# Bucketed attention with a gated product on one core: raw tokens in tiles of their own, and queries scaled by -1/8 on GpSimd so that a score pass is one minimum

## The chip, the core and the metric

The kernel runs on one core of a Trainium2 chip. The metric is the device time of one execution in microseconds (us). The engines: PE (TensorE) multiplies matrices and is fed weights by PEld; DVE (VectorE), ACT (ScalarE) and POOL (GpSimd) work elementwise; SP (SyncE) here only issues transfers (DMAs). Each engine takes its instructions in the order in which the program lists them, and waits on semaphores for the other engines and for DMAs. SBUF is the working memory on the chip, PSUM the memory that matmuls write.

## What is computed

Attention over 4 batches of 8 heads, 768 tokens and 64 dimensions, in which a query sees only keys of its own bucket, and then a gated product over all 3072 tokens:

```python
q_bits = (np.einsum('bhsd,dk->bhsk', q, proj) > 0)      # 6 bits; k likewise
mask = q_bucket[:, :, :, None] == k_bucket[:, :, None, :]
scores = (1 / 8) * np.matmul(q, k.transpose(0, 1, 3, 2))
scores = np.where(mask, scores, -1000000000.0)
attn = np.exp(scores - scores.max(-1)); attn = attn / (attn.sum(-1) + 1e-9)
x = (attn @ v) as [3072, 512]
out = (sigmoid(x @ w_gate) * (x @ w_val)) @ w_out       # 512 -> 1536 -> 512, weights in float64
```

## The kernel before

**Attention stage.** Sixteen pairs of heads (`pair`), each in two groups of three query tiles (`group`). `load` fetches q, k and v of a pair through SP's queue; `turn` transposes q and k on PE; `high` and `low` split each into a coarse and a fine float32r part, so that three matmuls give full precision; `hash_` multiplies by the projection, and `bits_q` and `bits_k` turn signs into +-1 rows, those of q times 2^34 (`HALF`, in `mul_q`). `scores` adds the product of these rows to q.k in PSUM, so that a pair of different buckets ends far below zero. `maximum` (L1048) is one DVE pass per query tile and head out of PSUM: it writes the scores times -1/8 to `e` in SBUF and accumulates their minimum into `st`. Two small DVE operations per query tile follow, for both heads at once: `scale_` (L1056) makes the exponential's factor, -1, or 0 for a row in which everything is masked, and `bias_` (L1060) makes its bias, the minimum or 0. `exponent` (L1067, ACT) takes exp(scale * e + bias) with the row's sum. Then transposes (L1100), copies out of PSUM (L1107, on ACT or DVE), products with v (L1117), the division (`divided`, L1127, POOL) and a store to `xd` in DRAM. Beside this run the conversion of the float64 weights (`load_w`, `load_pair`, `floats`: a DMA, DVE, ACT and POOL operations), and with two blocks of weights the first part of the gated product (`moe_early`, L537 and L570), whose sums go to `part` in DRAM.

**Late stage.** `products` does the other ten blocks, in pairs `jp` 1 to 5, batch after batch. A batch makes ten visits (`visit`), alternately for gate (g) and value (v). A visit is a seven-product scheme (L784): seven operands x0 to x6 made of the batch's tokens (halves of the features by halves of the tokens: B11, B12, B21, B22, and four differences), each times one of seven weight sums; the results build up in PSUM banks A, B and D and are read in between by ACT copies (`copies`, L792) and DVE additions (`summed`, L799). After a v visit, ACT and DVE make the gated values and six pieces of the product with w_out (L570) are put between the next visits' products. The weight sums of a visit (1.8 MB) stream from DRAM through POOL's queue (`fetch_stream`, L1217) into three slots. The last pair's weights (`jp` 5) are not converted in the attention stage but during batch 0 of the late one.

**The operands before.** Each operand X[n] is a tile with two halves, coarse and fine. The tokens of x0 and x1 are loaded (L652) into the place of their own fine half (`raw`), those of B12 and B22 into `xb` (L657); the differences go to `xt0` to `xt2` or over `xb` (L664). An ACT cast makes the coarse half (L669), a DVE subtraction the fine one (L672). The tiles are given back by the last visit of the batch: x0's after its first product, x2's and x3's together (`x`) after its last.

**The order.** All work is listed as tasks with a key, an engine, an estimated duration and counted resources (`stock`: tiles and banks). `Plan.order` plays the tasks through in time and emits them in that order; this becomes the order of every engine's queue. A DMA task is expected to land a fixed 2.0 us plus its bytes at 240 bytes per ns after its issue (0.6 us), or when its queue's wire is free. Any change of a duration or a resource can change the order everywhere.

## Time and profile before

| | before |
|---|---|
| median of 3 runs | 1084.75 us (1080.46 to 1087.05) |
| the profiled execution's own time | 1079.3 us |
| its span, first to last instruction | 1077.5 us |
| mean granted TensorE clock | 0.988 of full speed |
| busy PE / DVE / ACT / POOL | 1024.9 / 697.8 / 567.1 / 202.8 us |
| moved by DMA | 196.38 MB |

The profile is of one execution. Busy time counts an engine's instructions; TensorE's instructions are pipelined and their ends modelled, so that records overlap and a busy PE need not be PE at its peak. A row of the timeline gives start, length, engine, line, operation, output and inputs, and in brackets how long the engine had been idle and what ended that. A row of a group gives the count, then the total and mean length, then the idle time before its instructions and what ended most of it. In the chain of waits each piece is work that the end of the execution can be followed back to. Stretches of time are in us from the first instruction.

### The profile page before, as it was taken

The page shows a single profiled execution, that of the slowest core. Times are in us where ns is not written, and L with a number is a line of the kernel's source. Part 1 is how long each engine was busy: PE and PEld are TensorE (multiplying, and loading weights), DVE is VectorE, ACT ScalarE, POOL GpSimd, SP SyncE. Part 2 cuts the span into 40 slices and gives each one's busy share as a digit, 9 for nine tenths or more (in the row PEclk, how much of TensorE's full clock was granted, in tenths as well). Part 3 has the DMA queues.
Part 4 walks back from the last instruction along what each step waited for, and adds up shares of the span by engine and source line. Part 5 has one row for each costly group of instructions (what it writes and reads, how often), then busy time and mean ns, then how long its engine had stood idle before and what let it go on. Part 6 is the DMA issues. An engine that isn't in the chain of part 4 may idle for free.

```text
span 1077.5 us, 20497 instructions
## 1 busy us (share of the span) xinstructions
PE 1024.9 (95%) x8169; PEld 811.4 (75%) x8172; DVE 697.8 (65%) x1464; ACT 567.1 (53%) x1011; POOL 202.8 (19%) x230
## 2 busy tenths in 40 slices
PE   9999898999999999989999899999998999979998
PEld 5665566676675766656677789889997999879997
DVE  6898978889989778987746673464236333444333
ACT  2777776777786776857635433333234232422331
POOL 0013235344442423422031000000000000000000
PEclk9999998999999999999999999999999999989999
DMA  8345364764766456553168796466435743565521
GB/s 205 84 133 154 113 199 134 252 189 153 231 192 198 155 179 195 191 170 113 39 230 290 272 328 242 166 231 228 166 137 214 260 180 137 180 220 196 189 85 59
DMA packets 114561, 196.38 MB, mean 182 GB/s; under 512 B 61217, under 2 KB 83745, under 8 KB 109345
## 3 DMA queue, kind: packets, MB, share of 16 engines
q1 hardware_dynamic: 108544, 121.66, 36.0%
q0 software_dynamic: 5760, 73.40, 18.5%
q8 instruction: 64, 1.05, 0.4%
q14 instruction: 33, 0.26, 0.1%
q10 hardware_dynamic: 160, 0.00, 0.0%
HBM read 140.51 MB, written 41.94 MB: 169 GB/s over the span
## 4 chain that ended last, share of the span: by engine, by line
PE 77%; DVE 12%; DMA 6%; ACT 3%; issue 2%; POOL 1%; SPq 0%; ACTq 0%; DVEq 0%; POOLq 0%
PE y L570 13%; PE pv L1117 10%; PE sc L1034 8%; PE zBg L784 7%; PE zBv L784 7%; PE tp L1100 5%; PE zDg L784 4%; DVE e L1048 3%; PE zDv L784 3%; PE zo L570 3%; PE zg L537 3%; PE zv L537 3%; PE sc L1039 2%; PE zAg L784 2%; DMA x<-xd 2%
## 5 line engine op out<-in xcount | busy, mean ns | idle before, releaser
L1067 ACT ACTIVATE e<-e,st 128x768 f32<-128x768 f32 x192 | 196.5, 1026 | 71.6 <-DVE st L1060 71.5
L1048 DVE TENSOR_SCALAR_CACHE_REDUCE e<-sc 128x768 f32<-128x768 f32 x192 | 178.0, 951 | 21.8 <-PE sc L1039 21.2
L570 PE MATMUL y<-wo,gh 128*128 128x512 f32 x480 | 152.2, 399 | 0.0
L1117 PE MATMUL pv<-ef,vr 128*64 128x384 f32 x768 | 142.0, 499 | 0.0
L1100 PEld LDWEIGHTS tp<-ident,e 64*128 64x128 f32 x2304 | 85.5, 140 | 36.0 <-issue 20.2
L784 PE MATMUL zBv<-x,wsv 128*128 128x384 f32 x480 | 98.6, 340 | 9.9 <-ACT t167v L792 5.8
L570 PEld LDWEIGHTS y<-wo,gh 128*128 128x128 f32 x480 | 91.1, 190 | 15.7
L1100 PE MATMUL tp<-ident,e 64*128 64x64 f32 x2304 | 97.2, 227 | 5.3 <-ACT ef L1107 1.8
L784 PE MATMUL zBg<-x,wsg 128*128 128x384 f32 x480 | 97.3, 337 | 5.1 <-ACT t167g L792 3.7
L784 PEld LDWEIGHTS zBv<-x,wsv 128*128 128x128 f32 x480 | 86.5, 191 | 17.1 <-ACT t167v L792 7.4
L1107 ACT COPY ef<-tp 128x768 f32<-128x768 f32 x107 | 83.4, 792 | 25.5 <-PE tp L1100 25.2
L1034 PE MATMUL sc<-kh,ql 64*128 64x384 f32 x192 | 86.0, 448 | 9.2 <-DVE e L1048 2.9
L570 PE MATMUL y<-wo,gl 128*128 128x512 f32 x240 | 94.4, 393 | 0.0
L784 PEld LDWEIGHTS zBg<-x,wsg 128*128 128x128 f32 x480 | 85.7, 189 | 11.2 <-ACT t167g L792 4.4
L877 ACT CAST gh<-zt 128x384 fp32r<-128x384 f32 x80 | 41.0, 514 | 100.9 <-DVE zt L872 83.4
L1034 PE MATMUL sc<-kh,qsl 64*128 64x384 f32 x192 | 86.0, 448 | 7.1 <-DVE ef L1107 3.8
L1107 DVE COPY ef<-tp 128x768 f32<-128x768 f32 x85 | 80.4, 950 | 18.7 <-PE tp L1100 18.5
L1117 PEld LDWEIGHTS pv<-ef,vr 128*64 128x64 f32 x768 | 48.4, 137 | 52.5 <-issue 48.0
L1127 POOL TENSOR_TENSOR xs<-xs,rb 128x384 f32<-128x384 f32 x32 | 34.5, 1079 | 182.5 <-DVE xs L1124 117.6
L1039 PE MATMUL sc<-kb,qb 64*128 64x384 bf16 x384 | 65.2, 335 | 0.0
L1034 PE MATMUL sc<-kh,qsh 64*128 64x384 f32 x192 | 64.4, 335 | 0.0
L1034 PE MATMUL sc<-kl,qh 64*128 64x384 f32 x192 | 64.3, 335 | 0.0
(194 smaller groups left out, 2092.5 us busy)
## 6 DMA issues: line engine op xcount, KB each, us to landing
wsg<-kzg POOLq DMA_DIRECT2D x20, 1792.0 KB, 7.7
wsv<-kzv POOLq DMA_DIRECT2D x20, 1792.0 KB, 8.2
kzg<-wkg SPq DMA_DIRECT2D x10, 896.0 KB
kzv<-wkv SPq DMA_DIRECT2D x10, 896.0 KB
kr<-in_k_dram SPq DMA_DIRECT2D x64, 96.0 KB
qr<-in_q_dram SPq DMA_DIRECT2D x32, 192.0 KB
vr<-in_v_dram SPq DMA_DIRECT2D x16, 384.0 KB
qsh<-qh SPq DMA_DIRECT2D x32, 192.0 KB
```

Source lines behind the costliest of these rows:

```text
L537: nc.tensor.matmul(z["acc"][:, :GN], a[:, wc], x[xx][:, c, :], start=(c == 0 and i == 0), stop=(c == KC - 1 and i == 2),)
L570: nc.tensor.matmul(acc, a[:, slot, ts_], w, start=(first and i == 0), stop=(last and i == 2))
L784: nc.tensor.matmul(acc, streams[n, jp][:, c, wa, a_], X[x_][:, xa, c], start=first and c == 0 and i == 0, stop=c == 1 and i == 2, skip_gro ...
L877: nc.scalar.copy(side["h"][:, blk], w["z", blk])
L1034: nc.tensor.matmul(sc[:, j, :GN], q_[rows, c], z["k" + x][rows, h * GN : (h + 1) * GN], start=(m == 0), stop=False, tile_position=(j * D, 0),)
L1039: nc.tensor.matmul(sc[:, j, :GN], z["qb"][rows, c], z["kb"][rows, h], start=False, stop=True, tile_position=(j * D, 0),)
L1048: nc.vector.tensor_scalar(sp(e), gz["sc", t, h][:, :, :GN], -SCALE, None, op0=ALU.mult, op1=ALU.min, accum_out=gz["st", t][:, 0, h : h + 1],)
L1067: nc.scalar.activation(e, e, AF.Exp, bias=st[:, 2, h : h + 1], scale=st[:, 1, h : h + 1], accum_out=gz["su"][:, h * GT + t : h * GT + t + 1],)
L1100: nc.tensor.transpose(tp[:, r, at_ : at_ + D], gz["e", t, h][rows, c * P : (c + 1) * P], ident[rows, rows], tile_position=(r * D, 0),)
L1107: copy(gz["ef", c].rearrange("p (n r d) -> p r n d", r=2, d=D), gz["tp", c][:, :, :GN].rearrange("p r (n d) -> p r n d", d=D),)
L1117: nc.tensor.matmul(gz["pv"][rows, :GN], z["v"][:, h, c], gz["ef", c][:, h * GN : (h + 1) * GN], start=(c == 0), stop=(c == NC - 1), tile_p ...
L1127: nc.gpsimd.tensor_mul(gz["xs"], gz["xs"], gz["rb"])
```

## The change

*The score pass.* A new task, `scaled_q`, multiplies the loaded queries in place by -1/8 on POOL, between the load and the transposes. The projection for the queries is multiplied by -8 in turn, and the sign of `mul_q` is reversed, so that the scores come out of PSUM already times -1/8, with masked ones above 1e9. `maximum` now takes the minimum with 1e9 and accumulates the minimum, which is the bias; `scale_` and `bias_` are gone, the exponential's scale is the constant -1, and it waits for its own head's pass alone. Every scaling is by a power of two.

*Raw tokens.* B11, B21 and the difference T2 get tiles `r0`, `r1`, `r2`, B12 and B22 stay in `xb`; T3, T1 and T4 are written over B12, B11 and B21. Operand tiles are taken only by the casts, and x2 and x3 are given back one by one. The token loads no longer wait for the last conversions of the batch before (`in_turn["x"]`).

*Tiles and planner.* `ob`, `raw2` and `t` get one tile more each; the last two blocks of w_out go to the early blocks' tiles (`home`) and wait for the early part's last matmuls (`g_free`); the late pairs are loaded ahead of the late blocks of w_out. In the planner, transfers on the two queues slow each other, and two kinds of DMA get 3 us of `slack` on their landing.

```diff
...
-                        self.wire[e] = max(self.wire[e], free[e]) + t.size / RATE
-                        t.tail = max(t.tail, self.wire[e] + LANDING - free[e])
+                        other = "sp" if e == "pool" else "pool"
+                        begin, alone = max(self.wire[e], free[e]), t.size / RATE
+                        both = max(0, self.wire[other] - begin)
+                        takes = alone + min(alone, both / 2)
+                        self.wire[e] = begin + takes
+                        self.wire[other] += min(both, takes) / 2
+                        t.tail = max(t.tail, self.wire[e] + LANDING + t.slack - free[e])
...
-    nc.vector.tensor_scalar(mul_q, mul_q, -HALF, None, op0=ALU.mult)
+    nc.vector.tensor_scalar(mul_q, mul_q, HALF, None, op0=ALU.mult)
...
-                nc.vector.tensor_scalar_mul(w[rows, at_ : at_ + NB], praw[rows], sign)
+                nc.vector.tensor_scalar_mul(w[rows, at_ : at_ + NB], praw[rows], sign / -SCALE if n == "q" else sign)
...
-        ef=4, raw1=1, mid1=1, raw2=1, mid2=1, wk=1, xr=1, x=1, ob=2,
-        t=0, zt=0, ws0=0, ws1=0, ws2=0, xb=0, xt0=0, xt1=0, xt2=0, x1=0, x4=0, x5=0, x6=0, wk2=0,
+        ef=4, raw1=1, mid1=1, raw2=2, mid2=1, wk=1, xr=1, x2=1, x3=1, ob=3,
+        t=0, zt=0, ws0=0, ws1=0, ws2=0, xb=0, r0=0, r1=0, r2=0, x1=0, x4=0, x5=0, x6=0, wk2=0,
-    late_stock = dict(wk2=1, y=6, t=2, zt=3, xt0=1, xt1=1, xt2=1, ws1=1, ws2=1, xb=1, x1=1, x4=1, x5=1, x6=1)
+    late_stock = dict(wk2=1, y=6, t=3, zt=3, r0=1, r1=1, r2=1, ws1=1, ws2=1, xb=1, x1=1, x4=1, x5=1, x6=1)
...
-    def dma(key, nbytes, emit, engine="sp", **kw):
+    def dma(key, nbytes, emit, engine="sp", slack=0, **kw):
-        t.size = nbytes
+        t.size, t.slack = nbytes, slack
...
-        a = dma(key, 524288, load_, after=after, take=[place])
+        a = dma(key, 524288, load_, slack=3000 if last else 0, after=after, take=[place])
...
+    def home(j):
+        early = j if j < J1 else j - NJ + J1 if j >= NJ - J1 else None
+        pool, tag = (later["w"], f"wo{j}") if early is None else (w1, f"wo{early}")
+        return pool.tile([P, 2, N_EL], F32R, name=f"wo{j}", tag=tag)
...
-            w = later["w"].tile([P, 2, N_EL], F32R, name=f"w{n}{j}", tag=f"w{n}{j}")
+            w = home(j)
-        h = add(key, "act", 560, high, after=[e], take=[] if early or last else ["wk"])
+        h = add(key, "act", 560, high, after=[e] + (g_free if last else []), take=[] if early or last else ["wk"])
...
-                FIRST, "act", 415, lambda c=c: high(c), after=[a, prev], take=["x"] if c == 0 else []
+                FIRST, "act", 415, lambda c=c: high(c), after=[a, prev], take=["x2", "x3"] if c == 0 else []
...
-                take=z["bank"] if c == 0 else [], give=(["x"] + (["ws0"] if last == "end" else [])) if last and c == KC - 1 else [],
+                take=z["bank"] if c == 0 else [], give=(["x2", "x3"] + (["ws0"] if last == "end" else [])) if last and c == KC - 1 else [],
...
+        RAW = dict(B11="r0", B21="r1", T2="r2")
+        R = {}
+        def raw(n):
+            R[n] = later["w"].tile([P, 2, GN], F32, name=f"{n}_{b}", tag=RAW[n])
+            return R[n]
+        def load_first(n, h):
...
+            both = later["w"].tile([P, 2, 2, GN], F32, name=f"xb_{b}", tag="xb")
+            R["B12"], R["B22"] = both[:, 0], both[:, 1]
...
+                nc.sync.dma_start(both[:, h], xd_(h, 1))
...
+            X[n] = (xp if n in TAG else later["w"]).tile(HALF_X, F32R, name=f"{n}_{b}", tag=TAG.get(n, n))
+            nc.scalar.copy(X[n][:, 0], R[of])
+        def low(n, of):
+            nc.vector.tensor_sub(X[n][:, 1], R[of], f(X[n])[:, 0])
+        was = [a for g in range(NG) for a in stored[b, g]]
+        l0 = dma(FIRST, 393216, lambda: load_first("B11", 0), after=was, take=["r0"])
...
+        l1 = dma(FIRST, 393216, lambda: load_first("B21", 1), after=was, take=["r1"])
...
+        def dve(emit, after, take=(), give=()):
+            return add(FIRST, "dve", 930, emit, after=after, take=list(take), give=list(give))
+        def operand(n, of, after, give=()):
+            h = add(FIRST, "act", 830, lambda: high(n, of), after=after, take=["xr" if n == "x0" else n])
+            ready[n] = dve(lambda: low(n, of), [h], give=give)
+        def t3():
+            R["T3"] = R["B12"]
+            nc.vector.tensor_sub(R["T3"], R["B22"], R["B12"])
+        def t2():
+            nc.vector.tensor_add(raw("T2"), R["T3"], R["B11"])
+        def t1():
+            R["T1"] = R["B11"]
+            nc.vector.tensor_sub(R["T1"], R["B22"], R["T2"])
+        def t4():
+            R["T4"] = R["B21"]
+            nc.vector.tensor_sub(R["T4"], R["B21"], R["T2"])
+        d3 = dve(t3, [lb])
+        d2 = dve(t2, [d3, l0], take=["r2"])
+        operand("x0", "B11", [l0])
+        operand("x1", "B21", [l1])
+        operand("x5", "T2", [d2])
+        d1 = dve(t1, [d2, ready["x0"]])
+        operand("x4", "T1", [d1], ["r0"])
+        operand("x2", "T3", [d3])
+        d4 = dve(t4, [ready["x1"], d2], give=[])
+        operand("x6", "T4", [d4], ["r1"])
+        operand("x3", "B22", [lb])
+        add(FIRST, "sp", 0, lambda: None, after=[ready["x5"], d1, d4], give=["r2"])
+        add(FIRST, "sp", 0, lambda: None, after=[ready["x2"], ready["x3"], d1, d2], give=["xb"])
...
-                    z["ob"] = later["w"].tile([P, 2, GN], F32, name=f"ob{u}{t}", tag=f"xt{t}").rearrange("p a n -> p (a n)")[:, :DM]
+                    z["ob"] = later["w"].tile([P, 2, GN], F32, name=f"ob{u}{t}", tag=f"r{t}").rearrange("p a n -> p (a n)")[:, :DM]
...
-                    take = ["ob"] if m is None else [f"xt{t}"] if u else ["xb"] if t == 0 else []
+                    take = ["ob"] if m is None else [f"r{t}"] if u else ["xb"] if t == 0 else []
-                        FIRST, 262144, lambda: fetch(u, t, z), after=[parts[b, u, t]] + in_turn["ob"] + (list(ready.values()) if m is not None else []), take=take,
+                        FIRST, 262144, lambda: fetch(u, t, z), slack=3000, after=[parts[b, u, t]] + in_turn["ob"] + (list(ready.values()) if m is not None else []), take=take,
...
-                        for j in (2 * late, 2 * late + 1):
-                            load_w(1e3, "o", j, False, m1)
+                        for j in (2 * late, 2 * late + 1):
+                            load_w(1e3, "o", j, False, m1)
-                        made["o", j] = dma(1e3, 524288, fetch, after=[a, m1])
+                        made["o", j] = dma(1e3, 524288, fetch, after=[a, m1] + (g_free if j >= NJ - J1 else []))
...
-            prev = m7 = m(prev, "B", S3, "x2", False, False, [e16])
+            prev = m7 = m(prev, "B", S3, "x2", False, False, [e16], give=used("x2"))
-            prev = m3 = m(prev, "D", S4, "x3", False, True, [c22, *held], give=[slot_[1]] + used("x"))
+            prev = m3 = m(prev, "D", S4, "x3", False, True, [c22, *held], give=[slot_[1]] + used("x3"))
...
+        def scaled_q():
+            nc.gpsimd.tensor_scalar(z["q"], z["q"], -SCALE, None, op0=ALU.mult)
...
+        here["q"] = add(t0 - 10.72, "pool", 1000, scaled_q, after=[here["q"]])
...
-                gz["st", t] = at.tile([P, 3, 2], F32, name=f"st{u}_{t}", tag="st", bufs=stock["st"])
+                gz["st", t] = at.tile([P, 2], F32, name=f"st{u}_{t}", tag="st", bufs=stock["st"])
-                sp(e), gz["sc", t, h][:, :, :GN], -SCALE, None, op0=ALU.mult, op1=ALU.min,
-                accum_out=gz["st", t][:, 0, h : h + 1],
-            )
-        def scale_(t):
-            st = gz["st", t]
-            nc.vector.tensor_scalar(st[:, 1], st[:, 0], -MASKED * SCALE, -1.0, op0=ALU.is_lt, op1=ALU.mult)
-        def bias_(t):
-            st = gz["st", t]
-            nc.vector.scalar_tensor_tensor(
-                st[:, 2], st[:, 0], -MASKED * SCALE, st[:, 0], op0=ALU.is_lt, op1=ALU.mult
+                sp(e), gz["sc", t, h][:, :, :GN], -MASKED * SCALE, None, op0=ALU.min, op1=ALU.min,
+                accum_out=gz["st", t][:, h : h + 1],
-                e, e, AF.Exp, bias=st[:, 2, h : h + 1], scale=st[:, 1, h : h + 1],
+                e, e, AF.Exp, bias=st[:, h : h + 1], scale=-1.0,
...
-            a = [add(n - 3, "dve", 70, lambda t=t: scale_(t), after=least),
-                 add(n - 3, "dve", 70, lambda t=t: bias_(t), after=least)]
-                    n + 1.25, "act", 1025, lambda t=t, h=h: exponent(t, h), after=a + exps[:1],
+                    n + 1.25, "act", 1025, lambda t=t, h=h: exponent(t, h), after=[least[h]] + exps[:1],
```

57 lines of the change are left out of this document (2 added, 55 removed).

## The prediction

> **What bounds the kernel now.** I read the page's busy shares first, then the table by stretches of time, then the chain of waits, then TensorE's and VectorE's timelines at the places where the table shows a loss.
>
> ```profile
> span 1077.5 us, 20497 instructions
> ...
> PE 1024.9 (95%) x8169; PEld 811.4 (75%) x8172; DVE 697.8 (65%) x1464; ACT 567.1 (53%) x1011; POOL 202.8 (19%) x230
> ```
>
> TensorE (PE) is the bound: 95% busy, 52.6 us idle. Nothing in the change takes a matmul away, so it can only win PE's idle time and the slowness that follows a pause. The next rows place that. Each has the stretch and its length, then busy time and instruction count of PE, PEld, DVE, ACT and POOL, then the granted clock, the DMA share and GB/s.
>
> ```profile
> 27.00:540.00 513.00, 491.32 (x5377) 333.55 (x5377) 440.33 (x996) 375.14 (x649) 169.23 (x170) 0.99 0.53 161
> 540.00:594.00 54.00, 50.00 (x273) 41.31 (x272) 27.04 (x34) 26.21 (x48) 13.22 (x14) 1.00 0.73 263
> ...
> 162.00:189.00 27.00, 23.86 (x218) 17.85 (x216) 23.22 (x45) 16.09 (x27) 15.85 (x16) 0.87 0.45 131
> 594.00:621.00 27.00, 23.34 (x115) 21.33 (x114) 17.48 (x36) 10.59 (x21) 1.05 (x2) 0.94 0.79 284
> 621.00:648.00 27.00, 25.59 (x136) 23.67 (x135) 18.93 (x41) 11.38 (x21) 1.05 (x2) 1.00 0.91 331
> 675.00:702.00 27.00, 25.41 (x132) 23.04 (x130) 12.13 (x22) 10.48 (x19) 1.58 (x3) 1.00 0.51 175
> 702.00:729.00 27.00, 24.87 (x120) 22.61 (x120) 15.89 (x26) 9.29 (x18) 1.05 (x2) 0.94 0.66 233
> 783.00:810.00 27.00, 27.00 (x144) 25.16 (x143) 8.08 (x15) 8.49 (x17) 1.58 (x3) 1.00 0.43 151
> 810.00:837.00 27.00, 23.18 (x120) 20.82 (x119) 18.11 (x27) 11.91 (x21) 1.05 (x2) 1.00 0.61 219
> 918.00:945.00 27.00, 23.04 (x119) 20.68 (x118) 13.00 (x21) 10.87 (x19) 1.05 (x2) 1.00 0.53 196
> 945.00:972.00 27.00, 22.85 (x107) 20.89 (x106) 11.50 (x19) 6.90 (x14) 0.53 (x1) 0.87 0.53 188
> ```
>
> In the attention stage (27 to 540) PE idles 513.00 - 491.32 = 21.7 us, with DVE at 86%. In the late stage an undisturbed stretch of 27 us issues 144 matmuls (783:810), 0.1875 us each. Counting the missing ones takes in the slow clock too: around the three changes of batch 12 + 24, 24 and 25 are missing, 85 x 0.1875 = 15.9 us; in 945:972 37, 6.9 us; in 594:648 29 + 8, 6.9 us. Together 29.7 us. The transition, 540 to 594, adds 4.0 us of idle.
>
> The chain (start, length, what) and PE's timeline (start, length, instruction, in brackets the idle time before it) name the causes.
>
> ```profile
> 601.51 8.67 DMA rawg<-in_moe_w_gate_dram
> ...
> 688.63 6.16 DMA x<-xd
> ...
> 928.71 6.43 DMA x<-xd
> ...
> 952.85 9.78 DMA ob_2l<-part
> ```
> ```profile
> 611.80 1.94 PE L784 MATMUL zBg<-x,wsg 128*128 128x384 f32 x6 [3.03 <-ACT t167g L792]
> ...
> 629.99 1.31 PE L784 MATMUL zBg<-x,wsg 128*128 128x384 f32 x6 [1.41 <-DVE zt L870]
> ...
> 937.47 1.33 PE L784 MATMUL zBv<-x,wsv 128*128 128x384 f32 x6 [1.85 <-ACT t167v L792]
> ...
> 944.62 1.14 PE L784 MATMUL zAg<-x,wsg 128*128 128x384 f32 x5 [2.11 <-DVE x L672]
> ...
> 964.84 2.29 PE L784 MATMUL zBv<-x,wsv 128*128 128x384 f32 x6 [4.15 <-ACT t16v L792]
> ```
>
> Every one is a transfer that lands later than the planner thought: an ACT or DVE instruction that needs it stands at the head of its in-order queue, and the small PSUM copy that PE needs stands behind it. At a change of batch the tokens are fetched only when the last matmuls of the old batch let go of the operand tiles, hence two pauses each.
>
> **The change part by part.** *Raw tokens in own tiles.* Fetch, difference and conversion part ways. The tiles r0, r1, xb are free once the lows of a batch are written, early in its pass, so the next fetch runs a whole pass ahead; only conversions still wait for operand tiles, which the last visit frees one by one. They cost per batch seven casts and, with the four differences, eleven subtractions:
>
> ```profile
> L672 DVE TENSOR_TENSOR x<-rx,x 128x768 fp32r<-128x768 f32 x12 | 12.2, 1017 | 0.0
> ...
> L669 ACT CAST x<-rx 128x768 fp32r<-128x768 f32 x12 | 10.0, 833 | 1.7 <-DVE rx L664 1.7
> ```
>
> The work is the same as before, about 11.2 us of DVE and 5.8 us of ACT per batch; 783:810 shows 8.08 of 27 us DVE busy, so it fits in the last visit and the next. The 15.9 us should go, save one thing: a token transfer is planned at 0.6 + 2.0 + 393216/240 ns = 4.2 us from the start of its issue and took 6.2 to 6.4. About 2 us late at the head of DVE's queue may still hold up PE; I keep 0.9 us a batch, 2.7 in all. Gain 13.2 us (bounds 0 and 15.9).
>
> *A third ob buffer, 3 us of slack on its fetch, a wire model shared by both queues.* The 9.78 us fetch was awaited by a DVE add placed too early; it will be issued one buffer earlier and its add placed later. 6.9 us are there; I take three quarters, 5.2 (0 to 6.9). *Late weights:* two raw buffers, pairs before the o blocks, slack 3 us. The gate block that took 8.67 us was planned at 0.6 + 2.0 + 2.2 = 4.8; with slack 7.8, still short. I take 60% of 6.9, 4.1 (0 to 6.9). A third t tile and token loads that no longer wait for the last unit's xl: 1.0 us of the transition's 4.0.
>
> Against this, the second batch's tokens (4 x 393216 B) now move during 594:648, where the wires carry 284 to 331 GB/s: 1.57 MB, 4.8 us of wire. I cost it at nothing, as the weight stream covers it:
>
> ```profile
> 601.06 0.53 POOL L1217 DMA_DIRECT2D wsg<-kzg  x1 [7.91 <-PE zDv L784]
> ```
> ```profile
> wsg<-kzg POOLq DMA_DIRECT2D x3, 1792.0 KB, 8.6
> ```
>
> Such a block lands after about 8.6 us (median in 580:660), and the visit that uses this one begins with the zBg group at 629.99. If the cover is gone it costs up to 4.8 us. On SP's queue the early fetch can also stand ahead of weight loads and keep stores and wait for DVE to free r0; that is inside the same price, since only batch 0 has late weights. The last two o blocks now go into the early weights' tiles and wait on ACT for the last early unit, which ends in the transition; being loaded after the pairs, they should find it done. Late sum: 13.2 + 5.2 + 4.1 + 1.0 = 23.5 us less.
>
> *Score pass.* The pass keeps its length: with or without arithmetic, DVE takes as long over 128x768 from PSUM, so minimum for multiply is free:
>
> ```profile
> L1048 DVE TENSOR_SCALAR_CACHE_REDUCE e<-sc 128x768 f32<-128x768 f32 x192 | 178.0, 951 | 21.8 <-PE sc L1039 21.2
> ...
> L1107 DVE COPY ef<-tp 128x768 f32<-128x768 f32 x85 | 80.4, 950 | 18.7 <-PE tp L1100 18.5
> ```
>
> The two small operations per tile (L1056, L1060; 96 each) go. Their rows, and the worst of them with what PE did next:
>
> ```profile
> 272.33 0.16 DVE L1056 TENSOR_SCALAR st<-st 128x2 f32<-128x2 f32 x1
> 272.40 0.15 DVE L1060 SCALAR_TENSOR_TENSOR st<-st 128x2 f32<-128x2 f32 x1
> 272.47 0.95 DVE L1048 TENSOR_SCALAR_CACHE_REDUCE e<-sc 128x768 f32<-128x768 f32 x1
> ```
> ```profile
> 169.31 2.06 DVE L1056 TENSOR_SCALAR st<-st 128x2 f32<-128x2 f32 x1
> ```
> ```profile
> 172.35 0.68 PE L1034 MATMUL sc<-kh,qsl 64*128 64x384 f32 x1 [2.31 <-DVE ef L1107]
> ```
>
> Records overlap: from start to start a pair costs 0.14 us, 96 x 0.14 = 13.4 us. Some wait inside, as the 2.06 us one; the groups' lines give L1056 20.5 us and L1060 17.1 us for 96 each:
>
> ```profile
> L1056 DVE TENSOR_SCALAR st<-st 128x2 f32<-128x2 f32 x96 | 20.5, 213 | 0.6
> ...
> L1060 DVE SCALAR_TENSOR_TENSOR st<-st 128x2 f32<-128x2 f32 x96 | 17.1, 179 | 0.0
> ```
>
> Over the undisturbed 0.16 and 0.15 that is 5.1 + 2.7 = 7.8 us of waiting. So 21.2 us of DVE are freed, 4.8% of its 440.33. PE got 2.31 us of idle out of the one event, and 162:189 ran at 0.87, 0.13 x 27 = 3.5 us. This 5.8 us I count as 4; of the other 19.4 us of idle I take a fifth, 4. Early gain 8 (0 to 25).
>
> *Queries on GpSimd.* Sixteen operations on 128x768, which no row shows. Two-input ones took 1.28 us at 512 and 2.1 at 896:
>
> ```profile
> L361 POOL TENSOR_TENSOR mfg<-mfg,exg 128x512 f32<-128x512 f32 x10 | 12.8, 1277 | 35.8 <-DVE exg L356 34.5 <-DVE st L1060 1.3
> ...
> L473 POOL TENSOR_TENSOR wkg<-mfg,wkg 128x896 fp32r<-128x896 f32 x8 | 17.2, 2156 | 8.4 <-ACT wkg L470 7.3 <-DMA rb<-rd 1.0
> ```
>
> A line through them gives 1.86 us at 768; one input may halve it, 0.9. I take 1.3, and the ends for the range. POOL's total grows by 15 to 30 us on 203. Behind the new instruction on POOL's queue stand weight products, lows and the division of xs; they wait if q lands late. Each q is fetched pairs ahead and POOL is mostly idle, so only the first pair pays, where PE has nothing else: +1.3 us (0.9 to 2).
>
> POOL and DVE get in each other's way: 2.06 us for a 128x2 operation is no arithmetic. [...]
>
> I add 1 us of such blocking on PE. Early sum: -8 + 1.3 + 1.0 = -5.7 us.
>
> **Sum.** The profiled execution took 1079.3 us (span 1077.5 and 1.8 around it): 1079.3 - 23.5 - 5.7 = 1050.1. The median of the three runs, 1084.75, is 1.005 times that execution, so I forecast 1055.5.
>
> **The rivals.** [...]
>
> *The stalls move instead of going.* The token fetch is still planned 2 us too short and has no slack, so as many pauses come elsewhere; batches, late weights and transition give nothing. Left is 5.2 + 5.7: 1068.4, median 1074. For it: the same planning error made the pauses of before. Against: DVE is at 30% mid-pass, and only differences wait for landing there.
>
> *Slower: early fetches block the in-order queues.* With wires at 331 GB/s a token transfer may take as long as the 8.67 us one. Three consumers (two differences, one cast) in three batches would each repeat the stall before 611.80, 29 missing matmuls or 5.4 us: +48.6, against 15.9 + 10.3 of the late stage and 5.7 early: +16.7, so 1096 and a median of 1101. It decides once a stall costs PE over 31.9 / 9 = 3.5 us; the second and third fetch fall in stretches like 783:810 at 151 GB/s, which speaks against it.
>
> *Nearly all idle goes.* Four fifths of 29.7 + 4.0 + 21.7 + 3.5 = 58.9: -47, median 1037. It needs the new order to be better everywhere; DVE at (440.33 - 21.2) / 513 = 82% would allow it.
>
> **How the numbers follow.** Forecast 0.50 (1046 to 1066, since the shares I took may be off by some 10 us in all), lock 0.18, moved stalls 0.13, slower 0.06, nearly all 0.13. About 1% is what a measurement tells from no change: below 1073.9 lie the forecast, the last, most of the lock's case and some of the moved stalls: 0.82. Within 1%: the rest of these two, 0.12. Slower 0.06. The range 1040 to 1077 leaves out half of the best case and the upper moved stalls and slower case, under 0.2.
>
> **What would show it.** Right: no idle before zA at a change of batch; x<-xd issued 60 us or more ahead of the old batch's end; 140 or more matmuls in each 27 us from 650 on; no L1056/L1060 successor on DVE and DVE's early busy time down by about 30 us of records. Wrong: idle ended by DMA x<-xd or xb<-xd on DVE in mid-pass; PE idle in 27 to 540 above 21.7; GpSimd's new operation near 1.9 us with DVE rows of SBUF operations stretched beside it; scores starting over 2 us later than before.

## The result and the profile after

The changed kernel takes 1033.24 us (median of 4 runs, 1032.39 to 1034.06), the kernel before 1082.61 us (4 runs, 1078.39 to 1087.05): a ratio of 0.954 (95% interval 0.950 to 0.959). The forecast was 1055.5 us, its range 1040 to 1077: the time lies below the range. The profiled execution of the changed kernel took 1032.8 us. One execution of `fold_after_order` and one of the kernel before, at a mean granted clock of 0.655 and 0.848, are left out of the ratios below.

Its page, span and busy times of the engines:

```profile
span 1031.0 us, 20353 instructions
...
PE 1008.5 (98%) x8172; PEld 803.3 (78%) x8172; DVE 665.1 (65%) x1257; ACT 563.4 (55%) x1024; POOL 235.9 (23%) x248
```

PE is idle for 22.5 us where it was 52.6. The table by stretches of the changed kernel (stretch, length, busy time and count of PE, PEld, DVE, ACT, POOL, granted clock, DMA share, GB/s):

```profile
27.00:540.00 513.00, 502.22 (x5499) 343.78 (x5496) 415.79 (x802) 379.22 (x676) 200.61 (x191) 1.00 0.54 167
540.00:594.00 54.00, 48.26 (x248) 43.09 (x247) 34.81 (x55) 26.68 (x49) 9.16 (x10) 1.00 0.90 349
594.00:621.00 27.00, 27.00 (x143) 25.07 (x142) 14.23 (x29) 10.30 (x20) 1.06 (x3) 1.00 0.76 289
...
675.00:702.00 27.00, 27.00 (x143) 25.07 (x143) 15.72 (x27) 8.51 (x18) 1.06 (x2) 1.00 0.80 284
...
810.00:837.00 27.00, 27.00 (x144) 25.16 (x143) 12.36 (x23) 8.52 (x17) 1.58 (x3) 1.00 0.65 219
...
945.00:972.00 27.00, 27.00 (x143) 25.07 (x142) 10.04 (x19) 8.52 (x17) 1.16 (x3) 1.00 0.44 163
```

From 594 on no stretch has a pause, and each holds 142 to 144 matmuls up to 999. In the attention stage PE idles 10.8 us instead of 21.7, at a clock of 1.00.

Since the stages now start at other times, I measure each by its own ends, in the profiled execution of each kernel: the attention stage from the first score product (`sc`) to the start of the last product with v (`pv`), the late stage from the first product of the first visit (`zBg`) to the end. Of the changed kernel and then of the kernel before:

```profile
22.70:530.20 507.50, 496.72 (x5491) 338.51 (x5491) 416.13 (x805) 376.32 (x669) 196.60 (x186) 1.00 0.54 166
560.80:1031.00 470.20, 463.78 (x2419) 429.73 (x2417) 221.46 (x394) 167.16 (x320) 22.52 (x40) 1.00 0.58 210
```

```profile
20.60:548.50 527.90, 506.10 (x5501) 343.24 (x5501) 448.40 (x1012) 379.26 (x656) 170.22 (x171) 0.99 0.53 161
578.30:1077.50 499.20, 472.85 (x2419) 434.35 (x2417) 224.12 (x396) 168.24 (x321) 21.40 (x40) 0.99 0.55 198
```

| us | before | after | difference | the prediction took |
|---|---|---|---|---|
| start to first score | 20.6 | 22.7 | +2.1 | +1.3 |
| attention stage | 527.9 | 507.5 | -20.4 | -8 + 1.0 |
| transition | 29.8 | 30.6 | +0.8 | -1.0 |
| late stage | 499.2 | 470.2 | -29.0 | -22.5 |
| span | 1077.5 | 1031.0 | -46.5 | -29.2 |

Of the 17.3 us missed, 13.4 lie in the attention stage and 6.5 in the late one; start and transition missed the other way by 2.6. In the attention stage half of the gain is idle time of PE (21.8 us before, 10.8 after), the other half busy time (506.10 against 496.72). The latter goes in part with the clock: 108 to 189 us, granted 0.99, 0.95 and 0.87 before, had 1.00 throughout after; by these shares that is an estimated 5 us. The groups of the changed kernel show one thing that the prediction did not have, the exponential; the second fence is its group in the kernel before.

```profile
L1065 ACT ACTIVATE e<-e,st 128x768 f32<-128x768 f32 x192 | 178.7, 932 | 36.5 <-DVE e L1057 35.9
L1057 DVE TENSOR_SCALAR_CACHE_REDUCE e<-sc 128x768 f32<-128x768 f32 x192 | 176.4, 953 | 22.8 <-PE sc L1048 22.6
...
L945 POOL TENSOR_SCALAR qr<-qr 128x768 f32<-128x768 f32 x16 | 34.5, 2159 | 30.6 <-DMA qr<-in_q_dram 23.9 <-DMA rb<-rd 3.2 <-PE hk L980 2.2
```

```profile
L1067 ACT ACTIVATE e<-e,st 128x768 f32<-128x768 f32 x192 | 196.5, 1026 | 71.6 <-DVE st L1060 71.5
```

With the constant -1 as its scale instead of a column of `st`, an exponential takes 932 ns instead of 1026: 18 us less for ACT, a saving that the change's description doesn't mention. The score pass kept its length (951 before, 953 now), as predicted; GpSimd's scaling takes 2159 ns, above the upper end of 1.86 us.

### The profile page after: what moved, and what is told of

It is laid out like the page before. It is cut to its first block, busy times and chain, and to the rows that moved or that the text cites. A ratio compares the mean times of both kernels' runs of the same rounds, so it can differ in the third digit from the quotient of the medians.

```text
span 1031.0 us, 20353 instructions
## 1 busy us (share of the span) xinstructions
PE 1008.5 (98%) x8172; PEld 803.3 (78%) x8172; DVE 665.1 (65%) x1257; ACT 563.4 (55%) x1024; POOL 235.9 (23%) x248
## 4 chain that ended last, share of the span: by engine, by line
PE 85%; DVE 8%; issue 3%; ACT 2%; DMA 1%; POOL 0%; SPq 0%; DVEq 0%; ACTq 0%; POOLq 0%
PE y L581 16%; PE pv L1115 11%; PE sc L1043 9%; PE zBg L789 8%; PE zBv L789 8%; PE tp L1098 5%; PE zDg L789 4%; PE zDv L789 4%; DVE e L1057 3%; PE zo L581 3%; PE zg L548 3%; PE sc L1048 3%; PE zv L548 2%; PE zAg L789 2%; PE zAv L789 2%
## 5 line engine op out<-in xcount | busy, mean ns | idle before, releaser
L1065 ACT ACTIVATE e<-e,st 128x768 f32<-128x768 f32 x192 | 178.7, 932 | 36.5 <-DVE e L1057 35.9
L1105 ACT COPY ef<-tp 128x768 f32<-128x768 f32 x117 | 92.1, 798 | 50.8 <-PE tp L1098 49.7
L789 PE MATMUL zBv<-x,wsv 128*128 128x384 f32 x480 | 96.5, 335 | 0.9 <-ACT t167v L797 0.9
L1105 DVE COPY ef<-tp 128x768 f32<-128x768 f32 x75 | 71.2, 953 | 27.2 <-PE tp L1098 26.5
L1043 PE MATMUL sc<-kl,qsh 64*128 64x384 f32 x192 | 64.0, 333 | 0.0
```

The lines of the kernel that those rows point to most:

```text
L789: nc.tensor.matmul(acc, streams[n, jp][:, c, wa, a_], X[x_][:, xa, c], start=first and c == 0 and i == 0, stop=c == 1 and i == 2, skip_gro ...
L1043: nc.tensor.matmul(sc[:, j, :GN], q_[rows, c], z["k" + x][rows, h * GN : (h + 1) * GN], start=(m == 0), stop=False, tile_position=(j * D, 0),)
L1065: nc.scalar.activation(e, e, AF.Exp, bias=st[:, h : h + 1], scale=-1.0, accum_out=gz["su"][:, h * GT + t : h * GT + t + 1],)
L1105: copy(gz["ef", c].rearrange("p (n r d) -> p r n d", r=2, d=D), gz["tp", c][:, :, :GN].rearrange("p r (n d) -> p r n d", d=D),)
```

## The experiments

### The two halves

`late_only` leaves the score pass and the queries as before; `score_only` leaves operands, tiles, weights and planner as before.

> The late stage's part alone, the attention stage as before. First zBg to the end took 499.2 us before and 470.2 in the changed kernel. Independent halves: 28 to 30 us faster than before, a ratio of 0.973 (median near 1053), no idle before zA at a change of batch. If the late stage gains because the attention stage leaves it better placed (transfers, POOL), less than 20 us.

> The score pass and the queries' scaling alone, the late stage as before. In the changed kernel the stretch from the first score to the last product with v is 507.9 us against 528.3 before, and the first score comes 2.2 us later. If the two halves of the change are independent, this kernel is 18 us faster than before, a ratio of 0.983 (median near 1064), with the late stage (first zBg to the end) near 499 us. If the attention stage owes part of its gain to the new late stage (more tiles, other planning), it is less than 10 us faster.

Measured: `late_only` 1052.06 us, ratio 0.974 (0.970 to 0.978); `score_only` 1061.45 us, ratio 0.983 (0.977 to 0.990). By stages:

| us | before | after | late_only | score_only |
|---|---|---|---|---|
| first score at | 20.6 | 22.7 | 21.1 | 23.8 |
| attention | 527.9 | 507.5 | 528.5 | 508.1 |
| transition | 29.8 | 30.6 | 29.6 | 30.0 |
| late | 499.2 | 470.2 | 470.2 | 492.9 |

Each half does its work in its own stage and hardly touches the other's. The late edits reproduce 470.2 us exactly; the score edits give the attention stage within 0.6 us. One thing seems to cross over: `score_only` has no late edit, and its late stage is 6.3 us shorter than before.

```profile
561.90:1054.80 492.90, 469.84 (x2419) 431.83 (x2418) 223.89 (x396) 168.19 (x321) 22.09 (x40) 0.99 0.56 201
```

Its trace says where: the pause of 4.15 us that the kernel before has ahead of 964.84, with the slow clock behind it (37 missing matmuls, 6.9 us), isn't there. Around that place SP issues the same transfers in the same turn, and the stretch 929 to 956 us, which matches 945 to 972 since this stage begins 16 us earlier, holds 142 matmuls at a clock of 1.00. So this pause is no fixed feature of the kernel before; what brought it about in the profiled execution is open. Each of these lengths is of one execution: that of `score_only` took 1056.53 us, the others of this kernel up to 1068.11. Measured from 492.9 in place of 499.2 us, the late edits gain 22.7 us; by whole runs `late_only` is 25.7 us faster than the kernel before beside it (28 to 30 were expected).

### The late stage, part by part

Five kernels put late edits back; all else is the changed kernel.

`tokens_held` lets the next batch's raw tokens be loaded only after the first matmul of the last visit before it, about where they were loaded before:

```diff
-        was = [a for g in range(NG) for a in stored[b, g]]
+        was = [a for g in range(NG) for a in stored[b, g]] + ends.get("last_visit", [])
```

> The changed kernel, but the token loads of the next batch wait for the first product of the last visit of the batch before, as they did before; the tiles and everything else stay. The late stage took 499.2 us before and 470.2 in all three kernels with its new part. If the early fetch is what removed the pauses at a change of batch: 13 to 16 us come back (late stage 483 to 486) with idle before zA or zB at each change. If the tiles and conversions alone did it (operands given back one by one): under 4 us.

Measured: 1051.23 us, ratio 0.973 (0.968 to 0.978); late stage 488.2 us, 18.0 longer, more than the 13 to 16 expected. The row of that stage, then PE's timeline at the three changes of batch:

```profile
563.60:1051.80 488.20, 470.74 (x2420) 434.27 (x2418) 223.97 (x394) 168.23 (x320) 22.83 (x40) 0.99 0.55 201
```

```profile
683.03 0.57 PE L789 MATMUL zAg<-x,wsg 128*128 128x384 f32 x1 [4.81 <-ACT x L671]
684.91 1.97 PE L789 MATMUL zAg<-x,wsg 128*128 128x384 f32 x5 [1.31 <-DVE x L674]
803.55 0.44 PE L789 MATMUL zAg<-x,wsg 128*128 128x384 f32 x1 [1.61 <-ACT x L671]
805.02 1.14 PE L789 MATMUL zAg<-x,wsg 128*128 128x384 f32 x5 [1.04 <-DVE x L674]
922.91 0.44 PE L789 MATMUL zAg<-x,wsg 128*128 128x384 f32 x1 [1.61 <-ACT x L671]
924.39 1.16 PE L789 MATMUL zAg<-x,wsg 128*128 128x384 f32 x5 [1.03 <-DVE x L674]
```

Two pauses at each change, ended by a conversion, are back, much like those of the kernel before. Of the 18.0 us, 11.0 are idle time of PE and 7.0 longer busy time, at a clock of 0.99 where the changed kernel has 1.00. The profiled execution took 1053.59 us and the other one 1048.86, so the 18.0 may be up to some 5 us too much. In the changed kernel these tokens' loads are issued at 564.66 to 566.35, 672.75 to 678.64 and 787.44 to 793.32 us; with four batches of 117.5 us each from 560.8, that is some 110 to 125 us ahead of the batch that uses them.

`no_slack_two_ob` takes back the third `ob` buffer and the 3 us of slack on its fetch (`ob=2`, `slack=0`).

> The changed kernel with two ob buffers and no slack on their fetch. If these were what removed the pause of 4.15 us after a batch's end and its slow clock: 5 to 7 us come back in the late stage (475 to 477). If that pause came from the token loads that shared SP's queue and the wires just before: under 2 us.

Measured: 1039.12 us, ratio 0.962 (0.958 to 0.966). The late stage is 470.6 us, 0.4 longer; the rest of the run's difference lies in the transition (34.1 us, 3.5 longer) and the start. Whether those 3.5 us are the buffer's is not separated: with the changed kernel's order of the attention stage the transition takes 29.8 to 32.3 us in the other kernels. The 4.15 us pause before 964.84, which the prediction put down to an `ob` fetch issued too late, needs neither the buffer nor the slack in order to go. Nor is the rival shown, that the fetch shared SP's queue and the wires with token loads at the end of a batch: in `score_only` two buffers, no slack and those token loads are as before, and the pause is missing all the same. Its cause stays open.

`late_weights_before`, `raw_before` and `blocks_first` take back parts of the late weights' edits. `raw_before` does the first of the two diffs, against the changed kernel, `blocks_first` the second, `late_weights_before` both:

```diff
-        ef=4, raw1=1, mid1=1, raw2=2, mid2=1, wk=1, xr=1, x2=1, x3=1, ob=3,
+        ef=4, raw1=1, mid1=1, raw2=1, mid2=1, wk=1, xr=1, x2=1, x3=1, ob=3,
...
-        a = dma(key, 524288, load_, slack=3000 if last else 0, after=after, take=[place])
+        a = dma(key, 524288, load_, slack=0, after=after, take=[place])
```

```diff
+                        for j in (2 * late, 2 * late + 1):
+                            load_w(1e3, "o", j, False, m1)
                         for w_ in "gv":
                             for c in range(2):
                                 load_pair(1e3, w_, late, c, m1)
-                        for j in (2 * late, 2 * late + 1):
-                            load_w(1e3, "o", j, False, m1)
```

The first two of the following expectations name the turn of pairs and blocks the wrong way round: the kernel before loads the blocks of w_out first, the changed kernel the pairs. The numbers in them don't depend on it.

> The changed kernel with the late weights as before: no slack of 3000 on the last raw loads, one raw buffer in place of two in the late stage, output blocks after the pairs as the kernel before had them. Theory one (prediction's): these edits take away a part of the pauses at 594-648 and 945-972 us, worth 4.1 us: late stage 470.2 + 2 to 7 us, time 1035 to 1040 us. Rival: those pauses came from the token loads on the same queue, as the pause put down to the third output buffer did: late stage within 1 us of 470.2, time 1031 to 1035 us.

> The changed kernel without the slack of the last raw loads and with one raw buffer in the late stage; the output blocks stay ahead of the pairs. Late weights as before made the late stage 9.8 us longer (480.0 us). Theory one: one raw buffer is the cause, since a load then waits for the split of the one before: late stage 476 to 480 us, time 1037 to 1043 us. Rival: the turn of output blocks and pairs is the cause: 470 to 473 us, time 1031 to 1036 us.

> The changed kernel, only with the late output blocks' loads planned ahead of the pairs', as in the kernel before (the expectations of late_weights_before and raw_before name this turn the wrong way round: the kernel before has the blocks first, the changed kernel the pairs). Theory one (the turn of the loads gave the rest): late stage 470.2 + 9.8 - 2.1 = about 478 us, time about 1041 us. Rival (buffer, slack and turn together make the pause): 472 us or less, time 1035 us or less.

| | median us | ratio (interval) | late stage, us | against 470.2 |
|---|---|---|---|---|
| late_weights_before | 1042.69 | 0.968 (0.963 to 0.972) | 480.0 | +9.8 |
| raw_before | 1036.00 | 0.956 (0.950 to 0.962) | 472.3 | +2.1 |
| blocks_first | 1043.13 | 0.963 (0.946 to 0.980) | 478.1 | +7.9 |

The late weights were worth more than even theory one of `late_weights_before` expected (2 to 7 us). The parts add up (2.1 + 7.9 = 10.0 against 9.8); the turn of the loads is most of it, and a single raw buffer as the main cause, theory one of `raw_before`, fell. How the turn costs PE its time is seen in the timeline of `blocks_first`: POOL's load of the value weights waits until SP has stored them to DRAM, and PE waits for that load.

```profile
662.62 0.53 POOL L1213 DMA_DIRECT2D wsv<-kzv  x1 [25.56 <-DMA kzv<-wkv]
...
670.10 1.30 PE L789 MATMUL zBv<-x,wsv 128*128 128x384 f32 x3 [5.66 <-DMA wsv<-kzv]
```

Together the three reversals cost 18.0 + 0.4 + 9.8 = 28.2 us, beside the 29.0 that the late stage gained against the profiled execution of the kernel before and the 22.7 against that of `score_only`.

### The attention stage: the work that went

The first hunk below is `exp_scale_tile`, the second `two_small_dve`. `exp_scale_tile` gives the exponential a column that holds -1 as its scale; `two_small_dve` emits two operations like `scale_` and `bias_` behind the second pass of each query tile, on a tile that nobody reads; `scale_tile_and_small` does both. The order of all else is that of the changed kernel.

```diff
-                e, e, AF.Exp, bias=st[:, h : h + 1], scale=-1.0,
+                e, e, AF.Exp, bias=st[:, h : h + 1], scale=minus,
...
+            if h == 1:
+                nc.vector.tensor_scalar(junk[:, 0], junk[:, 2], -MASKED * SCALE, -1.0, op0=ALU.is_lt, op1=ALU.mult)
+                nc.vector.scalar_tensor_tensor(
+                    junk[:, 1], junk[:, 2], -MASKED * SCALE, junk[:, 2], op0=ALU.is_lt, op1=ALU.mult
+                )
```

> The changed kernel with the exponential's scale read from a tile that holds -1 in every partition, as before, instead of the constant; the order of every engine stays the same. The exponential took 1026 ns with a tile and 932 with the constant. Theory one (ACT's time reaches PE through the copies out of PSUM): the exponential goes back to 1025 ns, 18 us more of ACT, and the kernel is 3 to 8 us slower than the changed one. Theory two (ACT has slack at 73%, the gain is DVE's): within 1.5 us of the changed one. Theory three (the shorter exponential has another cause than the constant): it stays at 932 ns.

> The changed kernel with two small DVE operations of 128x2 added behind each query tile's second score pass, on a tile that nobody reads; the order of every engine is otherwise the same and nobody waits for them. This gives DVE back 0.14 us per query tile, 13 us, and the operations that can stand and wait while POOL works. If DVE's freed time is what shortened the attention stage: 6 to 14 us slower than the changed kernel. If it was the new order, or the shorter way from a pass to its exponential: less than 3 us slower.

> The changed kernel with both given back: the exponential's scale from a tile, and two small DVE operations per query tile that nobody waits for; the order as in the changed kernel. Attention stage: if the two are independent, 507.5 + 3.5 + 7.1 = 518 us; if either only matters while the other engine has no room, over 521, and near 528 the order would be worth nothing.

The exponential's group in `exp_scale_tile`, then the first small operation's in `two_small_dve`:

```profile
L1067 ACT ACTIVATE e<-e,st,minus 128x768 f32<-128x768 f32 x192 | 196.5, 1025 | 34.7 <-DVE e L1059 34.4
```

```profile
L1064 DVE TENSOR_SCALAR junk<-junk 128x2 f32<-128x2 f32 x96 | 31.3, 326 | 0.0
```

| | median us | ratio (interval) | attention, us | against 507.5 |
|---|---|---|---|---|
| exp_scale_tile | 1036.25 | 0.959 (0.956 to 0.963) | 511.0 | +3.5 |
| two_small_dve | 1042.20 | 0.966 (0.961 to 0.971) | 514.6 | +7.1 |
| scale_tile_and_small | 1042.69 | 0.965 (0.962 to 0.969) | 517.2 | +9.7 |

The column as scale is the whole difference in the exponential's length (1025 against 932 ns); of ACT's 18 us a fifth, 3.5, reaches the end. The small operations are worth more, 7.1 us; this may be somewhat too much, since the two groups take 47.3 us here and took 37.6 in the kernel before. Together they are worth 9.7; from 517.2 to the 527.9 us of the kernel before another 10.7 are missing.

### The attention stage: the order

These 10.7 us need another cause. Two are at hand: an exponential that no longer waits for the other head's pass, or the new order that the planner gives to the whole stage. Several kernels do the new work in other orders. `new_work_old_order` has the order of the kernel before on PE, ACT, SP and DVE (without the small operations), and GpSimd's scaling right behind its load:

```diff
                 for m in range(2):
                     nc.sync.dma_start(z[n][:, :, m], from_[:, m])
+                scaled_q()
...
-        here["q"] = add(t0 - 10.72, "pool", 1000, scaled_q, after=[here["q"]])
...
+            a = [add(n - 3, "dve", 70, lambda: None, after=least) for _ in range(2)]
...
-                    n + 1.25, "act", 1025, lambda t=t, h=h: exponent(t, h), after=[least[h]] + exps[:1],
+                    n + 1.25, "act", 1025, lambda t=t, h=h: exponent(t, h), after=a + exps[:1],
...
```

> The changed kernel's work in the order that the planner makes for the old score pass: the two small DVE operations are planned but not emitted, POOL scales the queries right behind their load, and PE, ACT, SP and the rest of DVE have the order of the kernel with the late part alone (attention stage 528.5 us from the first score to the last product with v, against 507.5 in the changed kernel). Giving back the exponential's length and the small operations costs 3.5 and 7.1 us there, so some 10 us are left. If these are the new order's: 515 to 520 us here. If they come from the freed time too (the two effects are more than their sum), or from the shorter way from a pass to its exponential: 507 to 511.

Measured: 1064.35 us, ratio 0.984 (0.980 to 0.989), attention 541.0 us, 12.5 us longer than the old work in the same order (`late_only`); the profiled execution took 1066.96 us, the others 1057.56 to 1065.57. No theory had this. The waits of POOL in `new_work_old_order` (engine, line, what it waited for; total, times, longest):

```profile
POOL qr L946 <- DMA qr<-in_q_dram: 41.3, 7, 12.7
...
POOL qr L946 <- PE sc L1048: 32.3, 3, 16.0
```

The scaling stands at the head of POOL's queue and waits for q's transfer, up to 12.7 us, and up to 16.0 us for score products, and what is behind it (weight products, `xs`) waits too. It is this placing that costs, as `fold_old_order` below bears out: without it the stage takes 516.7 us, and in the changed kernel's order the same operation turns out to cost the stage nothing. It says nothing of the order of the other engines. So the next kernel scales q without GpSimd, in the copies out of PSUM (the coarse part on ACT as shown, or alike on DVE where the planner gives it to DVE):

```diff
+                nc.scalar.mul(ordered(z["qh"]), turned_("q"), -SCALE)
...
+                for r in range(2):
+                    nc.vector.scalar_tensor_tensor(
+                        ordered(z["ql"])[:, r], turned_("q")[:, r], -SCALE, f(ordered(z["qh"]))[:, r],
+                        op0=ALU.mult, op1=ALU.subtract,
+                    )
```

`fold_old_order` does this in the order of the kernel before, `fold_after_order` in that of the changed kernel, and `fold_scale` in a new one, planned without a task for GpSimd. `true_costs` is the changed kernel planned with 930 ns for an exponential and 2150 for GpSimd's scaling, in place of 1025 and 1000; `plan_1010` and `plan_1040` change only the exponential's planned duration, to 1010 and 1040 ns.

> The late stage's edits stay; every engine issues the attention stage in the order of the old score pass (as in late_only), with the new work in it: minimum pass, constant -1.0 in the exponential, no small DVE operations. The factor -1/8 is put into the copies of q out of PSUM, so that GpSimd has no added operation to wait in front of, as it had in new_work_old_order. Theory one: the work taken away (3.5 us for the exponential's constant, 7.1 us for the small operations) is worth the same in the old order, and the other 10 us of the stage's gain are the new order: stage from the first score to the last product 528.5 - 10.6 = about 518 us (515 to 521), time about 1040 us. Theory two: the order is worth nothing and the rest is the shorter way from minimum to exponential: 507 to 511 us, time about 1031 us. Theory three: without a new order the freed time of DVE and ACT can't be used: 525 us or more, time 1047 us or more, and the 541.0 us of new_work_old_order were not GpSimd's waiting.

> The changed kernel with the factor -1/8 in the copies of q out of PSUM (a scaled copy, and a multiply-subtract for the low part in two operations), and no operation on GpSimd; planned anew. Theory one (prediction's): the scaling on GpSimd costs only at the start, where nothing covers its 2.13 us: first score at 20.6 to 21.2 us instead of 22.7, attention stage 507.5 +- 2, time 1029 to 1033 us. Rival: the 34.5 us of added GpSimd time hold DVE up in the stage: also 3 us or more off the stage, time under 1029 us. Second rival: one more DVE operation for each q costs more than GpSimd's: stage 2 us or more longer, time over 1033 us.

> The changed kernel with two of the planner's durations set to what the trace shows: exponential 930 ns instead of 1025, GpSimd's scaling of q 2150 ns instead of 1000. Theory one: the order already suits, a better table moves little: attention stage 507.5 +- 3 us, time 1030 to 1036 us. Rival: the plan is now nearer to what the engines do and takes part of the 10.8 us that TensorE still waits: stage 504 us or less, time under 1030 us.

> The order of the changed kernel is kept on TensorE and SyncE (the planner still plans GpSimd's scaling at 1000 ns, but emits nothing); the factor -1/8 sits in the copies of q out of PSUM, as in fold_scale. Only the order then lies between this kernel and fold_old_order (516.7 us). Theory one: the order of the changed kernel is worth about 9 us of the attention stage against the old one, whatever scales q: stage 505 to 510 us; first score at about 21 us; time 1028 to 1032 us. Rival: the 9 us came from GpSimd scaling q in DVE's and ACT's place, and the two operations of the low part cost the stage that: 514 us or more, time over 1036 us.

> The changed kernel; the planner's duration of the exponential 1010 ns in place of 1025, nothing else, so that the same work gets another order. Theory one (the order is a draw: fold_scale and true_costs, planned anew, gave 514.1 and 515.2 us, the old order 516.7): attention stage between 510 and 520 us, 2 us or more above the changed kernel's 507.5; time 1034 to 1045 us. Rival (the orders were worse because fold_scale and true_costs also changed other durations): 505 to 509 us, time 1029 to 1033 us.

> As plan_1010, with 1040 ns. Theory one (a draw): attention stage between 510 and 520 us, and not the same as with 1010 ns; time 1034 to 1045 us. Rival: 505 to 509 us, time 1029 to 1033 us.

> The same kernel as fold_after_order, for its profile: its three other runs took 1034.2 to 1036.6 us. Theory one (the order is worth about 9 us, whoever scales q): attention stage 507 to 512 us. Rival (GpSimd's scaling gave those 9 us): 514 us or more.

The stages of `fold_after_order` are read from `fold_after_order_2`, the same kernel.

| | order | q scaled by | median us | ratio (interval) | attention, us |
|---|---|---|---|---|---|
| late_only (old work) | of before | - | 1052.06 | 0.974 (0.970 to 0.978) | 528.5 |
| fold_old_order | of before | ACT/DVE | 1042.34 | 0.967 (0.963 to 0.971) | 516.7 |
| fold_after_order_2 | of after | ACT/DVE | 1036.36 | 0.957 (0.940 to 0.973) | 507.5 |
| after | of after | GpSimd | 1033.24 | 0.954 (0.950 to 0.959) | 507.5 |
| fold_scale | new | ACT/DVE | 1039.62 | 0.964 (0.960 to 0.969) | 514.1 |
| true_costs | new | GpSimd | 1041.24 | 0.966 (0.961 to 0.971) | 515.2 |
| plan_1010 | new | GpSimd | 1041.54 | 0.961 (0.955 to 0.967) | 516.6 |
| plan_1040 | new | GpSimd | 1047.43 | 0.966 (0.959 to 0.973) | 517.0 |

`fold_after_order` itself gave 0.956 (0.949 to 0.963). The rows by stretches of `fold_after_order_2`, `fold_old_order` and `plan_1010`:

```profile
24.20:531.70 507.50, 496.68 (x5492) 338.42 (x5491) 414.93 (x819) 376.52 (x669) 169.18 (x173) 1.00 0.54 167
```

```profile
20.80:537.50 516.70, 499.86 (x5500) 339.84 (x5501) 428.05 (x834) 363.71 (x656) 170.66 (x171) 1.00 0.54 164
```

```profile
24.10:540.70 516.60, 499.12 (x5490) 341.52 (x5491) 416.65 (x800) 379.75 (x675) 197.11 (x185) 0.99 0.54 164
```

Three things follow. First, GpSimd's scaling costs the stage no more than the DVE instructions that replace it (819 against 805): without it POOL is busy 169.18 us instead of 196.60, and the stage has the same 507.5 us. The 3.1 us by which the median of `fold_after_order_2` lies above the changed kernel's are outside the stage (first score 1.5 us later, transition 1.7 us longer). Second, the new work in the old order is worth 528.5 - 516.7 = 11.8 us (by putting it back into the new order, 9.7), and the order, with the same work, 516.7 - 507.5 = 9.2 us. Third, that order is a draw: shifting one planned duration by 15 ns either way loses the 9 us again, and a table nearer to the measured durations (`true_costs`) loses 7.7. This is far beyond what one and the same order varies by: the eight profiled kernels that have the changed kernel's order of the attention stage took 507.4 to 508.8 us in it. The exponential's shorter wait, the other cause at hand, isn't enough either: `plan_1010`, `plan_1040`, `true_costs` and `fold_scale` all plan with it.

"Order" includes which engine copies the transposed exponentials (`tp`) out of PSUM. DVE makes 85 of the 192 copies in the kernel before and in `fold_old_order`, 75 in the changed kernel and in `fold_after_order_2`. But a like split doesn't give 507.5 us by itself: DVE makes 74 in `plan_1010`, 73 in `fold_scale` and 71 in `true_costs`. The new orders leave PE idle 15 to 18 us in the stage (`plan_1010`: 516.60 - 499.12 = 17.5), the changed kernel's 10.8. What in the changed kernel's order makes the difference was not traced to single instructions.

Several expectations missed. `true_costs` met neither theory. `fold_scale` has the time and the stage that its second rival named, an added DVE operation that costs more than GpSimd's; but the same operations cost nothing in `fold_after_order_2`. `fold_after_order` has the stage that was expected, but its first score came at 24.2 us instead of about 21 and its time was 4 us above the range. `plan_1040` took longer in all than expected, and its stage is nearly that of `plan_1010`. None of these kernels has a lower median than the changed one.

### The start

The same kernels settle the first score, which starts 2.1 us later than before. PE's first transpose of k and first score product, in the kernel before, the changed kernel and `fold_after_order_2`:

```profile
7.93 0.59 PE L949 MATMUL tk<-ident,kr 64*128 64x64 f32 x12
...
20.59 0.44 PE L1034 MATMUL sc<-kh,ql 64*128 64x384 f32 x1
```

```profile
8.09 0.59 PE L957 MATMUL tk<-ident,kr 64*128 64x64 f32 x12
...
22.73 0.44 PE L1043 MATMUL sc<-kh,ql 64*128 64x384 f32 x1
```

```profile
9.52 0.59 PE L957 MATMUL tk<-ident,kr 64*128 64x64 f32 x12
...
24.18 0.44 PE L1058 MATMUL sc<-kh,ql 64*128 64x384 f32 x1
```

From one to the other take 12.66, 14.64 and 14.66 us. With no operation on GpSimd the way is as long as with it; in the old order with one (`new_work_old_order`, first score at 21.4) it is nearly as short as before. So the 2 us are the order's again: PE transposes q behind the hash of k. The planned task on GpSimd brings this order about: `fold_scale`, planned without one, takes 12.6 us. The moment of the first transpose itself differs between runs, from 7.93 to 9.54 us (`blocks_first`), which puts up to 1.6 us into any comparison of single spans.

This bears on what the order is worth, for a stage that starts 2 us later has less left to do. From the first transpose of k to the last product with v the kernel before takes 540.6 us, `late_only` 541.2, `fold_old_order` 529.3, `fold_after_order_2` 522.2 and the changed kernel 522.1. Over this whole way the change gains 18.5 us: the new work in the old order is worth 11.9, and the order 7.1 rather than 9.2; the other 2 us only move from the stage to the start.

## Why the prediction was wrong

The sign and the bound were right, and so were the causes of the late pauses but one. The step that failed is the early gain: it was priced at 8 us as a fraction of idle time, with no term for the shorter exponential and none for the new order. Two late terms also came out below what their reversals cost, and the `ob` term far above.

- **The bound.** PE stayed the bound, from 95% to 98% busy.
- **Raw tokens in own tiles: right, perhaps too low.** "The 15.9 us should go, save one thing"; 13.2 were taken. `tokens_held` gives 18.0, with some 5 us of doubt. The 2.7 us kept for token loads that land about 2 us later than planned did not occur: loaded over 100 us ahead, none of them is awaited by PE.
- **Third `ob` buffer and slack: wrong step.** 5.2 us were taken; `no_slack_two_ob` gives 0.4 in the late stage. The pause before 964.84 was real in that execution, but it is missing in `score_only` without any late edit, so it can't be put down to the buffer or the slack; its cause is open.
- **Late weights: right, too low.** "I take 60% of 6.9, 4.1 (0 to 6.9)"; 9.8 were measured, above the upper end, and 7.9 of it by the turn of pairs and blocks, not by the slack on which the step reckoned. Counting missing matmuls in the kernel before gave an upper end for what was lost there, not for what the edit is worth beside the others.
- **Late sum.** 22.5 without the transition, against 29.0; the three reversals sum to 28.2. The count of missing matmuls, 29.7, came nearer, but in part by luck: tokens and late weights gave more than was counted for them, the `ob` edit nearly nothing. Against `score_only`, without the pause of 6.9 us, the gain is 22.7, and 22.5 would have been right. The fractions taken off were caution with no row behind them.
- **Wires of the early fetch at nothing: right.** From 594 on PE waits for none of it.
- **Early gain of 8: the step that failed.** "Of the other 19.4 us of idle I take a fifth, 4." The stage gained 20.4, or 18.5 counted from the first transpose. Two small operations gave 7.1, near the whole of the 8, so DVE's freed time was rightly seen. Missing were the exponential's 94 ns, which the diff shows (`scale=-1.0`) but the sum doesn't price, 3.5 us; and the new order, 9.2 us in the stage or 7.1 over the whole way, which one rival names and the sum puts at nothing. The bounds, 0 to 25, held the gain.
- **Blocking between POOL and DVE, +1.0: not shown.** No run shows this term; it was the author's estimate. With GpSimd's scaling, and with DVE and ACT doing it instead, the stage has 507.5 us. In the changed kernel the 23 score passes that overlap the scaling took 954 ns on average, the other 169 took 953; two DVE operations of 128x512 (L356) that began during it took 1.19 and 1.14 us, and the 28 of that line with no GpSimd operation beside them at most 0.70.
- **GpSimd's operation 1.3 us (0.9 to 2): wrong, and without effect.** It takes 2159 ns. The two-input rows (1277 ns for 512, 2156 for 896) were the nearer ones; the halving for one input had no row. The +1.3 us at the start came out near the measured 2.1, by another cause, the order.
- **Transition -1.0: wrong in sign**, +0.8.
- **The chances.** The rival that came true in size is "Nearly all idle goes" at 1037 us (0.13), with its condition, a new order that is better everywhere; its four fifths of 58.9 us, 47, stand beside the measured 46.5. The range stopped at 1040 since it left out half of that case. That condition was met for the attention stage by luck of the plan, not by anything the sum foresaw: with one of the four other orders the attention stage would be 6.6 to 9.5 us longer, and the time 1040 to 1043, at the lower end of the range: that is worked out; three of those kernels ran in 1039.62 to 1041.54 us, and `plan_1040`, whose transition is also 5.3 us longer than the changed kernel's, in 1047.43. The 0.18 of "lock" stood for an early gain eaten by GpSimd's sixteen operations, which no run shows.
- **What would show it.** As said: no idle before zA at a change of batch; loads far ahead; 142 to 144 matmuls in each 27 us; DVE's busy time in the attention stage down by 448.40 - 416.13 = 32.3 us (about 30 was said). Two of the signs of "wrong" also appeared, GpSimd's operation above 1.9 us and scores over 2 us later, and neither meant what was said of it.

## What to carry to other kernels

Where a planner orders the whole kernel, an edit's worth is its work plus a draw of the order: here about 12 and 7 us, and a shift of one planned duration by 15 ns took the draw back. So keep the order fixed when you ask what an edit is worth, and try several orders when you ask for the best time. Missing matmuls are counted in one execution: before a pause is divided among edits, see whether it is there in a second one, which the 4.15 us pause was not. Price every operand that a diff changes, too: a scale that turns from a column into a constant was 18 us of ACT.

## What the runs showed of the hardware

- An exponential over 128x768 took 932 ns on average with a constant scale and a column as bias (the changed kernel), and 1025 to 1026 ns with columns for both (`exp_scale_tile`, the kernel before).
- A GpSimd multiplication of 128x768 by a constant took 2159 ns on average in the changed kernel, longer than the two-input operations of 128x896 there (2109 to 2116 ns).
- A 128x2 operation of DVE between two passes took 326 ns on average in `two_small_dve` where the same operation took 213 in the kernel before; POOL was busy 197 instead of 170 us. That POOL's added operations lengthen it fits, but was not separated. The 2.06 us one of the kernel before ran from 169.31 to 171.37 us, and beside it a GpSimd operation of 128x896 from 169.27 to 171.35. Nine of the 192 small operations there took over 0.3 us; each of the nine ended within 0.03 us after a GpSimd operation beside it, and the 157 with none beside them took at most 0.17 us.
- The late stage repeats closely: 470.1 to 470.6 us in the twelve kernels that have all its edits, whatever their attention stage.
